# Longer stretches of one kind of matmul in a squared-relu FFN behind a dynamic convolution, and two relus of eight on VectorE

## The chip, the cores and the metric

The kernel runs on one core of one Trainium2 chip. The metric is the device time of one execution in microseconds (us). All times below are medians of several executions; the profiles are of one execution each, and their span (first to last instruction) lies about 2 us below the time of the same execution. The granted clock of a profile is the share of its full clock that TensorE was given; 1 is all of it.

The profile shows five engines of the core, working side by side (in the kernel before TensorE is busy for 98% of the span, ScalarE for 77% and VectorE for 74%): TensorE (PE in the profile; PEld is its loading of weights), VectorE (DVE), ScalarE (ACT), GpSimd (POOL) and SyncE (SP), which here only issues DMA transfers. Where an engine waits, the profile names what ended the wait. VectorE's order, which this case turns on, is that of the program. PSUM is the memory that the matmuls of this program write to and that ScalarE and VectorE read the results from.

## The reference

A softmax over 7 taps per token and head weights a causal convolution of `x`; its result goes through a feed-forward network with a squared relu. Cut to what matters:

```python
batch, seq, d_model = (8, 4096, 192);  n_heads, kernel_size = 8, 7;  d_ff = 2048
w   = softmax(weight_gen, axis=-1)                 # (8, 4096, 8, 7)
out = np.einsum('bshk,bskhg->bshg', w, x_unf)      # x_unf: the last 7 rows of x
x   = out.reshape(B * S, D)                        # (32768, 192)
h   = np.maximum(x @ w_in, 0.0)
return (h * h @ w_out).astype(np.float32)
```

## The kernel before

The 32768 tokens are worked in 64 blocks of 512. For each block TensorE does the convolution (conv) as a product of `x` with a banded matrix, then x @ w_in (MM1), then h*h @ w_out (MM2). MM1 of a block comes as eight pairs of 128-column chunks; each pair fills one PSUM tile of 128x1024 fp32 elements, and there are three such tiles (`ps_h`, bufs=3), shared with the conv. ScalarE takes the relu of a pair out of PSUM, VectorE squares it:

```python
def st_relu(j, fp):
    t1 = p_t1.tile([P, 2, 2, TH], f16, name="t1")
    nc.scalar.activation(out=t1, in_=h_t[(j, fp)], func=ActF.Relu)

def st_sq(j, fp):
    g = p_g.tile([P, 2, 2, TH], f16, name="g")
    nc.vector.tensor_tensor(out=g, in0=t1, in1=t1, op=AluOp.mult)
```

The banded matrices `bd` are made by VectorE: rows of softmax weights (`wr`), read back from device memory (`vd`), times a mask. `wr_load` is that read, issued by SyncE; `o_store`, the write of the finished output, is issued by SyncE too. This is the loop (`j` is the block, `fp` the pair; cut: some cases of the first blocks and the softmax; `#` comments added):

```python
for j in range(NBLK):
    ...
    st_conv(j + 1); st_y_evac(j + 1)
    st_bands(j + 2, 0)              # VectorE: bands for the conv after the next
    for fp in G0:                   # pairs 0..3
        st_mm1(j, fp); st_relu(j, fp); st_sq(j, fp)
    for half in (0, 1):
        st_mm2(j - 1, G1, (half,))  # second half of the block BEFORE
        o_copy(j - 1, half, nc.scalar.copy)
    o_store(j - 1, (0, 1), nc.sync) # in the middle of the block
    st_bands(j + 2, 1)
    ...                             # a part of a later softmax
    for fp in G1:                   # pairs 4..7
        st_mm1(j, fp); st_relu(j, fp); st_sq(j, fp)
    st_mm2(j, G0)
    if j + 3 < NBLK:
        wr_load(j + 3)              # last in the block
```

The softmax here doesn't subtract the row's maximum and nothing guards it: scores larger than these inputs give would overflow.

Of the kernel before, what the change touches and what calls it, by code (L numbers as in the profile page):

```python
# [9 lines left out]
def kernel(  # L10
# [20 lines left out]
    nc = tc.nc  # L31
# [41 lines left out]
    p_wr = ctx.enter_context(tc.tile_pool(name="p_wr", bufs=4))  # L73
    p_bd = ctx.enter_context(tc.tile_pool(name="p_bd", bufs=3))
    p_y = ctx.enter_context(tc.tile_pool(name="p_y", bufs=2))
    p_t1 = ctx.enter_context(tc.tile_pool(name="p_t1", bufs=5))
    p_g = ctx.enter_context(tc.tile_pool(name="p_g", bufs=10))
    p_os = ctx.enter_context(tc.tile_pool(name="p_os", bufs=2))
    p_dr = ctx.enter_context(tc.tile_pool(name="p_dr", bufs=3, space=bass.MemoryType.DRAM))
# [14 lines left out]
    def band_mask():  # L94

        nc.gpsimd.memset(mask, 1.0)
        for sign, base in ((1, 0), (-1, KK - 1)):
            nc.gpsimd.affine_select(
                out=mask, in_=mask, pattern=[[sign, P], [0, 2]], compare_op=AluOp.is_ge,
                fill=0.0, base=base, channel_multiplier=-sign,  # L100
            )
# [2 lines left out]


    WQ = 2
    w_sa, w_sb, wo_st, x_st = {}, {}, {}, {}

    def load_w_in(q):
        n = Dff // WQ  # L110
        c = slice(q * n, (q + 1) * n)
        w_sa[q] = p_st.tile([P, n], f32, name="w_sa")
        w_sb[q] = p_st.tile([P, n], f32, name="w_sb")
        nc.sync.dma_start(out=w_sa[q], in_=moe_w_in[0:P, c])
        for r0 in (0, RT):
            nc.sync.dma_start(out=w_sb[q][r0 : r0 + RT], in_=moe_w_in[P:D, c])

    def cast_w_in(q, straight, crossed):
        n = Dff // WQ
        c = slice(q * n, (q + 1) * n)  # L120
        straight(out=w_i[:, 0, c], in_=w_sa[q])
        crossed(out=w_i[RT:P, 1, c], in_=w_sa[q][0:RT])
        crossed(out=w_i[0:RT, 1, c], in_=w_sa[q][RT:P])
        straight(out=w_i[:, 2, c], in_=w_sb[q])

    def load_w_out(q):
        n = NF // WQ
        wo_st[q] = p_st.tile([P, n, Dm], f32, name="wo_st")
        nc.sync.dma_start(
            out=wo_st[q],  # L130
            in_=moe_w_out[q * n * P : (q + 1) * n * P].rearrange("(c p) m -> p c m", p=P),
        )

    def cast_w_out(q, copy):
        n = NF // WQ
        copy(out=w_o[:, q * n : (q + 1) * n], in_=wo_st[q])  # L136


    class Softmax:
# [113 lines left out]
    def x_load(j):  # L253
        x_t[j] = p_x.tile([P, NT, D], f16, name="xt")
        block_load(j, x_t[j], x[j // NBB], D, nc.gpsimd)

    def x_load_f32(j):
        x_st[j] = p_st.tile([P, NT, D], f32, name="x_st")
        block_load(j, x_st[j], x[j // NBB], D, nc.sync)

    def x_cast(j, copy):
        x_t[j] = p_x.tile([P, NT, D], f16, name="xt")
        copy(out=x_t[j], in_=x_st[j])

    def wr_load(j):
        wr_t[j] = p_wr.tile([P, NT, HP, SL * 2], f16, name="wr")
        wr = wr_t[j].rearrange("p t g c -> p t (g c)")
        block_load(j, wr, vd_t[j // NBB], H * SL, nc.sync)

    def wr_load_sbuf(s, order, engines):  # L270

        wr_t[0] = p_wr.tile([P, NT, HP, SL * 2], f16, name="wr")
        for n, i in enumerate(order):
            t0 = max(starts[i], 0)
            engines[n % len(engines)].dma_start(
                out=wr_t[0][:, i].rearrange("p g c -> p (g c)"),
                in_=s.v[t0 // s.r : (t0 + P) // s.r, HALO : HALO + s.r].rearrange(
                    "p r g c e -> p r (g c e)"
                ),
            )  # L280
# [91 lines left out]

    def st_mm2(j, fps, halves=(0, 1)):

        if fps[0] == 0:
            o_t[j] = [ps_o.tile([P, TB], f32, name=f"o{half}") for half in range(2)]
        o = o_t[j]
        for fp in fps:
            for jj in range(2):
                fc = 2 * fp + jj  # L380
                for half in halves:
                    for cc in range(2):
                        nc.tensor.matmul(  # L383
                            out=o[half][:, cc * Dm : (cc + 1) * Dm],
                            lhsT=g_t[(j, fp)][:, half, jj, cc * P : (cc + 1) * P],
                            rhs=w_o[:, fc, :],
                            start=(fc == 0 and cc == 0), stop=(fc == NF - 1),
                            skip_group_check=True,
                        )

    def st_relu(j, fp):
        t1 = p_t1.tile([P, 2, 2, TH], f16, name="t1")
        t1_t[(j, fp)] = t1
        nc.scalar.activation(out=t1, in_=h_t[(j, fp)], func=ActF.Relu)  # L394

    def st_sq(j, fp):
        g = p_g.tile([P, 2, 2, TH], f16, name="g")
        g_t[(j, fp)] = g
        t1 = t1_t[(j, fp)]
        nc.vector.tensor_tensor(out=g, in0=t1, in1=t1, op=AluOp.mult)  # L400

    def o_copy(j, half, copy):
        if half == 0:
# [17 lines left out]
            for tiles in (groups, ((NT - 1,),))[part]:  # L421
                st_band(j, tiles)

    G0, G1 = (0, 1, 2, 3), (4, 5, 6, 7)
    UNIT = 4

    with nc.allow_low_precision("fp16 matmul pipeline"), tc.manual_schedule():
# [12 lines left out]
        def spin(n):  # L440
            for i in range(n):
                nc.tensor.matmul(  # L442
                    out=wp[:, 0:TB], lhsT=warm[:, 0:P], rhs=warm, start=True, stop=True
                )

        spin(38)
        band_mask()
        nc.gpsimd.memset(v_first[2], 0.0)
        nc.gpsimd.memset(v_big, 0.0)
        vec, act, pool = nc.vector.tensor_copy, nc.scalar.copy, nc.gpsimd.tensor_copy  # L450

        def softmax(s, lo, hi):
            s.exp(lo, hi)
            s.recip(lo, hi)
            s.scale(lo, hi, nc.vector)

        s0, s1, s2 = parts
        s0.load(nc.sync)
        s1.load(nc.sync)
        x_load_f32(0)  # L460
        load_w_in(0)
        load_w_in(1)
        s0.exp(0, s0.rh)
        s1.exp(0, s1.rh)
        x_cast(0, act)
        s0.recip(0, s0.rh)
        s0.scale(0, s0.rh, nc.vector)
        s1.recip(0, s1.rh)
        wr_load_sbuf(s0, (0, 2, 1, 3, 4), (nc.scalar, nc.gpsimd))
        s0.store(nc.scalar)  # L470
        cast_w_in(0, act, pool)
        wr_load(1)
        x_load_f32(1)
        load_w_out(0)
        for i in (0, 2, 1, 3, 4):
            st_band(0, (i,))
        st_conv_alloc(0)
        st_conv(0)
        spin(4)
        st_y_evac(0)  # L480
        s1.scale(0, s1.rh, nc.vector)
        s1.store(nc.sync)
        cast_w_in(1, pool, pool)
        x_cast(1, pool)
        wr_load(2)
        x_load(2)
        load_w_out(1)
        for q in range(WQ):
            cast_w_out(q, pool)
        s2.load(nc.sync)  # L490
        st_bands(1, 0)
        st_bands(1, 1)


        plan = {}
# [16 lines left out]
        for j in range(NBLK):  # L512
            nb, lo, hi = plan.get(j, (None, 0, 0))
            after = plan.get(j + 1)
            if after and after[1] == 0:
                s = Softmax(after[0], 0, R, v_big, new_vd(after[0]))
                s.load(nc.sync)
                rows_of[after[0]] = s
            if j + 3 < NBLK:
                x_load(j + 3)  # L520

            late = j == 2
            if j:
                if j + 1 < NBLK:
                    st_conv_alloc(j + 1)
                    st_conv(j + 1)
                    st_y_evac(j + 1)
                if not late:
                    st_bands(j + 2, 0)
            for fp in G0:  # L530
                st_mm1(j, fp)
                st_relu(j, fp)
                st_sq(j, fp)
            if j:
                for half in (0, 1):
                    st_mm2(j - 1, G1, (half,))
                    o_copy(j - 1, half, nc.scalar.copy)
                o_store(j - 1, (0, 1), nc.sync)
            elif NBLK > 1:
                st_conv_alloc(1)  # L540
                st_conv(1)
                st_y_evac(1)
                st_bands(2, 0)
            if not late:
                st_bands(j + 2, 1)
            if hi and j:
                s = rows_of[nb]
                softmax(s, lo, hi)
                if hi == s.rh:
                    s.store(nc.sync)  # L550
            for fp in G1:
                st_mm1(j, fp)
                st_relu(j, fp)
                st_sq(j, fp)
            st_mm2(j, G0)
            if hi and not j:
                softmax(rows_of[nb], lo, hi)
            if late:
                st_bands(j + 2, 0)
                st_bands(j + 2, 1)  # L560
            if j + 3 < NBLK:
                wr_load(j + 3)
        st_mm2(NBLK - 1, G1, (0,))
        o_copy(NBLK - 1, 0, nc.scalar.copy)
        st_mm2(NBLK - 1, G1, (1,))
        o_store(NBLK - 1, (0,), nc.sync)
        o_copy(NBLK - 1, 1, nc.vector.tensor_copy)
        o_store(NBLK - 1, (1,), nc.scalar)
# [30 lines left out]
```

## Time and profile before

| | before |
|---|---|
| time, median of 3 (range) | 794.05 us (792.2 to 794.29) |
| span of the profile, granted TensorE clock | 791.0 us, 0.993 |
| TensorE busy | 773.3 us, 98% |
| ScalarE, VectorE busy | 77%, 74% |
| one block, conv to conv | 11.78 us, or 11.89 where ScalarE does a long exp for a later softmax |

TensorE is busy 98% of the time, at a clock of 0.993, so the span is its stream of instructions. The prediction below shows the lines.

### The profile page before, as it was taken

To read this page: it belongs to the slowest core of one execution; us is meant where nothing else is said; L and a number is where in the kernel's file an instruction comes from. 1 tells how busy PE (TensorE), PEld (TensorE's weight loads), DVE (VectorE), ACT (ScalarE), POOL (GpSimd) and SP (SyncE) were. 2 spreads that over 40 slices of the span, in tenths; PEclk is the share of its full clock that TensorE was granted. 3 is DMA by queue.
4 is the path that set the end of the run, shared out by engine and by line. 5 is a ranking of instruction groups with operands and counts; after the bars stand their busy time and mean duration, and the time that the engine had idled before them with its cause. 6 is when DMAs were issued, how large, how long until landed. Compare 5 with 4: busy or idle time off the path is not lost.

```text
span 791.0 us, 32666 instructions
## 1 busy us (share of the span) xinstructions
PE 773.3 (98%) x14890; PEld 679.7 (86%) x14890; DVE 586.7 (74%) x1040; ACT 605.4 (77%) x756; POOL 81.8 (10%) x98
## 2 busy tenths in 40 slices
PE   5998999999999999999999999999999999999998
PEld 2787888888888888888988888888888888888887
DVE  5888777777877768777778777877778777666653
ACT  3676877877877877877877877887787787787785
POOL 7501000010001000010001000011000010000000
PEclk9999999999999999999999999999999999999999
DMA  7862633435433543435433353333533334342111
GB/s 197 227 111 38 157 52 64 75 53 145 75 52 65 102 104 65 74 52 148 73 51 67 72 135 67 70 55 68 150 60 65 65 64 89 65 69 46 50 42 41
DMA packets 124009, 65.64 MB, mean 83 GB/s; under 512 B 84545, under 2 KB 121056, under 8 KB 123104
## 3 DMA queue, kind: packets, MB, share of 16 engines
q1 hardware_dynamic: 82032, 47.92, 21.6%
q0 software_dynamic: 40992, 15.28, 18.5%
q8 instruction: 116, 1.90, 1.1%
q10 hardware_dynamic: 848, 0.38, 0.2%
q14 instruction: 21, 0.17, 0.1%
HBM read 49.35 MB, written 29.36 MB: 100 GB/s over the span
## 4 chain that ended last, share of the span: by engine, by line
PE 93%; DMA 3%; DVE 2%; ACT 1%; issue 0%; SPq 0%; ACTq 0%; DVEq 0%
PE o L383 44%; PE h L364 43%; PE yp L339 6%; DMA wg<-in_weight_gen_dram 1%; DVE bd L290 1%; DMA wr<-v_first 1%; DMA x_st<-in_x_dram 1%; DMA vd<-v_first 0%; DVE g L400 0%; ACT t L394 0%; DVE v_big L194 0%; ACT ex L173 0%; DVE v_first L194 0%; DVE ssum L181 0%; DVE rcp L186 0%
## 5 line engine op out<-in xcount | busy, mean ns | idle before, releaser
L394 ACT ACTIVATE t<-h 128x1024 f16<-128x1024 f32 x512 | 482.8, 1031 | 9.4 <-PE h L364 8.8
L400 DVE TENSOR_TENSOR g<-t 128x1024 f16<-128x1024 f16 x512 | 346.9, 692 | 147.1 <-ACT t L394 146.9
L364 PE MATMUL h<-y,w_i 64*128 64x256 f16 x6144 | 362.5, 270 | 2.0 <-ACT y L352 1.2
L383 PE MATMUL o<-w_o,g 128*128 128x192 f16 x4096 | 360.0, 246 | 0.0
L383 PEld LDWEIGHTS <-g 128*128 128x128 f16 x4096 | 331.5, 98 | 26.8 <-DVE g L400 17.1
L364 PEld LDWEIGHTS <-w_i 64*128 64x128 f16 x6144 | 292.4, 94 | 51.0 <-issue 14.2
L290 DVE TENSOR_TENSOR bd<-wr,mask 128x1664 f16<-128x1664 f16 (+2 forms) x201 | 163.4, 844 | 11.2 <-DMA wr<-vd 6.2
L352 ACT CAST y<-yp 128x768 f16<-128x768 f32 x64 | 51.1, 798 | 122.8 <-PE yp L339 122.8
L251 POOL DMA_DIRECT2D xt<-in_x_dram x62 | 51.2, 826 | 460.4 <-PE yp L339 437.0
L405 ACT COPY o_sb<-o 128x384 f32<-128x384 f32 x127 | 62.9, 495 | 38.3 <-PE o L383 38.3
L339 PE MATMUL yp<-bd,xt 128*32 128x104 f16 (+13 forms) x4608 | 59.9, 203 | 10.6 <-DVE bd L290 10.5
L339 PEld LDWEIGHTS <-xt 128*32 128x32 f16 (+3 forms) x4608 | 51.2, 91 | 21.6 <-issue 21.5
L181 DVE TENSOR_REDUCE ssum<-ex 128x64 f32<-128x448 f32 (+6 forms) x49 | 25.9, 529 | 35.4 <-ACT ex L173 35.4
L194 DVE TENSOR_TENSOR v_big<-ex,rcp 128x112 f16<-128x112 f32 (+3 forms) x192 | 32.7, 234 | 1.6
L173 ACT ACTIVATE ex<-wg 128x448 f32<-128x448 f32 (+6 forms) x49 | 26.5, 541 | 5.0 <-DMA wg<-in_weight_gen_dram 4.9
L186 DVE RECIPROCAL rcp<-ssum 128x64 f32<-128x64 f32 (+6 forms) x49 | 23.3, 475 | 1.7
L245 POOL DMA_DIRECT2D xt<-in_x_dram x9 | 5.0, 552 | 85.2 <-PE yp L339 85.2
L442 PE MATMUL wp<-warm 128*128 128x512 f16 x42 | 12.4, 463 | 1.3 <-DVE warm L434 1.3
L241 POOL DMA_DIRECT2D xt<-in_x_dram x7 | 3.8, 541 | 77.5 <-PE yp L339 77.5
L442 PEld LDWEIGHTS <-warm 128*128 128x128 f16 x42 | 4.6, 114 | 7.9 <-issue 3.7
L194 DVE TENSOR_TENSOR v_first<-ex,rcp 128x112 f16<-128x112 f32 (+2 forms) x32 | 5.5, 242 | 0.2
L136 POOL CAST w_o<-wo_st 128x1536 f16<-128x1536 f32 x2 | 3.7, 1826 | 5.7 <-DMA wo_st<-in_moe_w_out_dram 5.7
(22 smaller groups left out, 25.5 us busy)
## 6 DMA issues: line engine op xcount, KB each, us to landing
out_dram<-o_sb SPq DMA_DIRECT2D x63, 384.0 KB, 2.8
xt<-in_x_dram POOLq DMA_DIRECT2D x46, 240.0 KB, 4.4
wg<-in_weight_gen_dram SPq DMA_DIRECT2D x6, 1064.0 KB, 6.0
wr<-vd SPq DMA_DIRECT2D x46, 80.0 KB, 3.0
vd<-v_big SPq DMA_DIRECT2D x7, 512.0 KB, 2.9
xt<-in_x_dram POOLq DMA_DIRECT2D x16, 192.0 KB, 3.9
wo_st<-in_moe_w_out_dram SPq DMA_DIRECT2D x2, 768.0 KB, 7.5
wr<-vd SPq DMA_DIRECT2D x17, 64.0 KB, 2.9
```

The source lines that it names most:

```text
L173: nc.scalar.activation(out=self.ex[:, lo:hi].rearrange("p r g k e -> p (r g) k e"), in_=self.wg[:, lo:hi].rearrange("p r (g e) k -> p (r g ...
L181: nc.vector.tensor_reduce(out=ssum.rearrange("p r g e -> p (r g) e"), in_=self.ex[:, lo:hi].rearrange("p r g k e -> p (r g) e k"), axis=Ax ...
L194: eng.tensor_tensor(out=bass.AP(tensor=v.tensor, offset=v.offset + lo * H * SL + lo % SL * 2 + g * SL * 2, ap=[list(v.ap[0]), [H * SL + 2, ...
L251: eng.dma_start(out=dst[:, first:last], in_=ap)
L290: nc.vector.tensor_tensor(out=bd_t[j][:, H * lo : H * hi].rearrange("p (g m c) -> p g m c", g=shape[1], c=2 * SL), in0=wr_t[j][:, i : tile ...
L339: nc.tensor.matmul(out=yp_t[j][p0 : p0 + m, col + a : col + b], lhsT=x_t[j][:, i, 32 * q : 32 * q + m], rhs=bd[:, h // 2, h % 2, a - lo : ...
L352: nc.scalar.copy(out=y, in_=yp_t[j][:, 0 : NK * TH].rearrange("p (k c) -> p k c", k=NK))
L364: nc.tensor.matmul(out=h[:, half, jj, :], lhsT=w_i[r0 : r0 + RT, slot, fc * P : (fc + 1) * P], rhs=y_t[j][r0 : r0 + RT, k, :], start=(jj = ...
L383: nc.tensor.matmul(out=o[half][:, cc * Dm : (cc + 1) * Dm], lhsT=g_t[(j, fp)][:, half, jj, cc * P : (cc + 1) * P], rhs=w_o[:, fc, :], star ...
L394: nc.scalar.activation(out=t1, in_=h_t[(j, fp)], func=ActF.Relu)
L400: nc.vector.tensor_tensor(out=g, in0=t1, in1=t1, op=AluOp.mult)
L405: copy(out=o_sb_t[j][:, half], in_=o_t[j][half][:, 0 : 2 * Dm])
```

## The change

Its intent is to lose less between kinds of matmul. Before, a block's stream is conv, MM1 (4 pairs), MM2 of the block before, MM1 (4 pairs), MM2: five changes of kind. After, it is conv, MM1 (8 pairs), MM2 (8 pairs): three. Since eight relus in a row would press ScalarE (there they follow at 0.915 us, the pairs of MM1 at 0.655, as the prediction reads from the trace before), VectorE takes the relus of pairs 1 and 4, and ScalarE squares those two. The first loads and casts are reordered as well. The core of the diff (the start, some 100 lines, is cut; so are the buffer counts):

```diff
     def st_relu(j, fp):
-        nc.scalar.activation(out=t1, in_=h_t[(j, fp)], func=ActF.Relu)
+        if swapped:
+            nc.vector.tensor_scalar_max(out=t1, in0=h_t[(j, fp)], scalar1=0.0)
+        else:
+            nc.scalar.activation(out=t1, in_=h_t[(j, fp)], func=ActF.Relu)
...
+    SWAPPED = (1, 4)
+    MM2 = (0, 2, 3, 5, 6, 7, 1, 4)
...
                 if not late:
                     st_bands(j + 2, 0)
-            for fp in G0:
+            for fp in range(NFP):
                 st_mm1(j, fp)
                 st_relu(j, fp)
-                st_sq(j, fp)
-            if j:
-                for half in (0, 1):
-                    st_mm2(j - 1, G1, (half,))
-                    o_copy(j - 1, half, nc.scalar.copy)
-                o_store(j - 1, (0, 1), nc.sync)
...
-            for fp in G1:
-                st_mm1(j, fp)
-                st_relu(j, fp)
+            for fp in SWAPPED:
                 st_sq(j, fp)
-            st_mm2(j, G0)
...
-            if j + 3 < NBLK:
-                wr_load(j + 3)
+            st_mm2(j, MM2[:4])
+            for half in (0, 1):
+                st_mm2(j, MM2[4:], (half,))
+                if more or half == 0:
+                    o_copy(j, half, nc.scalar.copy)
+            if more:
+                o_store(j, (0, 1), nc.sync)
+                if j + 3 < NBLK:
+                    wr_load(j + 3)
```

More of the change, by code (lines that the diff above doesn't have):

```diff
@@ L75 @@
     p_y = ctx.enter_context(tc.tile_pool(name="p_y", bufs=2))
-    p_t1 = ctx.enter_context(tc.tile_pool(name="p_t1", bufs=5))
+    p_t1 = ctx.enter_context(tc.tile_pool(name="p_t1", bufs=6))
+    p_t1s = ctx.enter_context(tc.tile_pool(name="p_t1s", bufs=2))
     p_g = ctx.enter_context(tc.tile_pool(name="p_g", bufs=10))
@@ L106, with cast_w_in, load_w_out @@
     WQ = 2
-    w_sa, w_sb, wo_st, x_st = {}, {}, {}, {}
+    NQ = Dff // WQ
+    w_sa, w_sb, x_st = {}, {}, {}
     def load_w_in(q):
-        n = Dff // WQ
-        c = slice(q * n, (q + 1) * n)
-        w_sa[q] = p_st.tile([P, n], f32, name="w_sa")
-        w_sb[q] = p_st.tile([P, n], f32, name="w_sb")
+        c = slice(q * NQ, (q + 1) * NQ)
+        w_sa[q] = p_st.tile([P, NQ], f32, name="w_sa")
+        w_sb[q] = p_st.tile([RT, NQ], f32, name="w_sb")
         nc.sync.dma_start(out=w_sa[q], in_=moe_w_in[0:P, c])
-        for r0 in (0, RT):
-            nc.sync.dma_start(out=w_sb[q][r0 : r0 + RT], in_=moe_w_in[P:D, c])
-    def cast_w_in(q, straight, crossed):
-        n = Dff // WQ
-        c = slice(q * n, (q + 1) * n)
-        straight(out=w_i[:, 0, c], in_=w_sa[q])
-        crossed(out=w_i[RT:P, 1, c], in_=w_sa[q][0:RT])
-        crossed(out=w_i[0:RT, 1, c], in_=w_sa[q][RT:P])
-        straight(out=w_i[:, 2, c], in_=w_sb[q])
-    def load_w_out(q):
-        n = NF // WQ
-        wo_st[q] = p_st.tile([P, n, Dm], f32, name="wo_st")
-        nc.sync.dma_start(
-            out=wo_st[q],
-            in_=moe_w_out[q * n * P : (q + 1) * n * P].rearrange("(c p) m -> p c m", p=P),
-        )
-    def cast_w_out(q, copy):
-        n = NF // WQ
-        copy(out=w_o[:, q * n : (q + 1) * n], in_=wo_st[q])
+        nc.sync.dma_start(out=w_sb[q], in_=moe_w_in[P:D, c])
+    def cast_w_in(q, op, copy):
+        c = slice(q * NQ, (q + 1) * NQ)
+        lower, upper = slice(0, RT), slice(RT, P)
+        out_p, slot, src = {
+            "straight": (slice(0, P), 0, w_sa[q]),
+            "up": (upper, 1, w_sa[q][lower]),
+            "down": (lower, 1, w_sa[q][upper]),
+            "last": (lower, 2, w_sb[q]),
+            "last up": (upper, 2, w_sb[q]),
+        }[op]
+        copy(out=w_i[out_p, slot, c], in_=src)
+    def load_w_out(q, n):
+        nc.gpsimd.dma_start(
+            out=w_o[:, q * NF // n : (q + 1) * NF // n],
+            in_=moe_w_out[q * Dff // n : (q + 1) * Dff // n].rearrange(
+                "(c p) m -> p c m", p=P
+            ),
+        )
     class Softmax:
@@ L268, in wr_load, with wr_load_sbuf @@
         block_load(j, wr, vd_t[j // NBB], H * SL, nc.sync)
-    def wr_load_sbuf(s, order, engines):
-        wr_t[0] = p_wr.tile([P, NT, HP, SL * 2], f16, name="wr")
+    def wr_load_sbuf(j, s, order, engines):
+        wr_t[j] = p_wr.tile([P, NT, HP, SL * 2], f16, name="wr")
         for n, i in enumerate(order):
-            t0 = max(starts[i], 0)
+            t0 = max(j * TB + tile_start(j, i), 0)
             engines[n % len(engines)].dma_start(
-                out=wr_t[0][:, i].rearrange("p g c -> p (g c)"),
+                out=wr_t[j][:, i].rearrange("p g c -> p (g c)"),
                 in_=s.v[t0 // s.r : (t0 + P) // s.r, HALO : HALO + s.r].rearrange(
@@ L373, in st_mm2 @@
     def st_mm2(j, fps, halves=(0, 1)):
-        if fps[0] == 0:
+        if fps[0] == MM2[0]:
             o_t[j] = [ps_o.tile([P, TB], f32, name=f"o{half}") for half in range(2)]
@@ L386, in st_mm2 @@
                             rhs=w_o[:, fc, :],
-                            start=(fc == 0 and cc == 0), stop=(fc == NF - 1),
+                            start=(fp == MM2[0] and jj == 0 and cc == 0),
+                            stop=(fp == MM2[-1] and jj == 1),
                             skip_group_check=True,
@@ L391, in st_relu @@
     def st_relu(j, fp):
-        t1 = p_t1.tile([P, 2, 2, TH], f16, name="t1")
+        swapped = fp in SWAPPED
+        t1 = (p_t1s if swapped else p_t1).tile([P, 2, 2, TH], f16, name="t1")
         t1_t[(j, fp)] = t1
-        nc.scalar.activation(out=t1, in_=h_t[(j, fp)], func=ActF.Relu)
+        if swapped:
+            nc.vector.tensor_scalar_max(out=t1, in0=h_t[(j, fp)], scalar1=0.0)
+        else:
+            nc.scalar.activation(out=t1, in_=h_t[(j, fp)], func=ActF.Relu)
     def st_sq(j, fp):
@@ L399, in st_sq @@
         t1 = t1_t[(j, fp)]
-        nc.vector.tensor_tensor(out=g, in0=t1, in1=t1, op=AluOp.mult)
+        if fp in SWAPPED:
+            nc.scalar.activation(out=g, in_=t1, func=ActF.Square)
+        else:
+            nc.vector.tensor_tensor(out=g, in0=t1, in1=t1, op=AluOp.mult)
     def o_copy(j, half, copy):
@@ L422, in st_bands @@
                 st_band(j, tiles)
-    G0, G1 = (0, 1, 2, 3), (4, 5, 6, 7)
+    SWAPPED = (1, 4)
+    MM2 = (0, 2, 3, 5, 6, 7, 1, 4)
     UNIT = 4
@@ L444, in spin @@
                 )
-        spin(38)
-        band_mask()
-        nc.gpsimd.memset(v_first[2], 0.0)
-        nc.gpsimd.memset(v_big, 0.0)
-        vec, act, pool = nc.vector.tensor_copy, nc.scalar.copy, nc.gpsimd.tensor_copy
         def softmax(s, lo, hi):
@@ L455, in softmax @@
             s.scale(lo, hi, nc.vector)
+        vec, act, pool = nc.vector.tensor_copy, nc.scalar.copy, nc.gpsimd.tensor_copy
         s0, s1, s2 = parts
+        spin(36)
+        band_mask()
         s0.load(nc.sync)
-        s1.load(nc.sync)
-        x_load_f32(0)
         load_w_in(0)
         load_w_in(1)
+        x_load_f32(0)
         s0.exp(0, s0.rh)
-        s1.exp(0, s1.rh)
-        x_cast(0, act)
         s0.recip(0, s0.rh)
         s0.scale(0, s0.rh, nc.vector)
-        s1.recip(0, s1.rh)
-        wr_load_sbuf(s0, (0, 2, 1, 3, 4), (nc.scalar, nc.gpsimd))
-        s0.store(nc.scalar)
-        cast_w_in(0, act, pool)
-        wr_load(1)
-        x_load_f32(1)
-        load_w_out(0)
+        cast_w_in(0, "straight", act)
+        cast_w_in(0, "up", act)
+        cast_w_in(0, "down", pool)
+        cast_w_in(0, "last", act)
+        cast_w_in(0, "last up", act)
+        wr_load_sbuf(0, s0, (0, 1, 2, 4, 3), (nc.sync, nc.gpsimd))
+        cast_w_in(1, "up", vec)
+        cast_w_in(1, "down", vec)
+        x_load(1)
+        s1.load(nc.sync)
+        for q in range(4):
+            load_w_out(q, 4)
+        nc.gpsimd.memset(v_first[2], 0.0)
+        x_cast(0, act)
+        wr_load_sbuf(1, s0, range(NT), (nc.sync,))
+        s0.store(nc.sync)
+        s2.load(nc.sync)
+        cast_w_in(1, "straight", act)
+        cast_w_in(1, "last", act)
         for i in (0, 2, 1, 3, 4):
@@ L479 @@
         spin(4)
+        s1.exp(0, s1.rh)
         st_y_evac(0)
+        cast_w_in(1, "last up", act)
+        x_load(2)
+        nc.gpsimd.memset(v_big, 0.0)
+        st_bands(1, 0)
+        st_bands(1, 1)
+        s1.recip(0, s1.rh)
         s1.scale(0, s1.rh, nc.vector)
         s1.store(nc.sync)
-        cast_w_in(1, pool, pool)
-        x_cast(1, pool)
         wr_load(2)
-        x_load(2)
-        load_w_out(1)
-        for q in range(WQ):
-            cast_w_out(q, pool)
-        s2.load(nc.sync)
-        st_bands(1, 0)
-        st_bands(1, 1)
         plan = {}
@@ L522 @@
             late = j == 2
+            more = j + 1 < NBLK
             if j:
-                if j + 1 < NBLK:
+                if more:
                     st_conv_alloc(j + 1)
@@ L529 @@
                     st_bands(j + 2, 0)
-            for fp in G0:
+            for fp in range(NFP):
                 st_mm1(j, fp)
                 st_relu(j, fp)
-                st_sq(j, fp)
-            if j:
-                for half in (0, 1):
-                    st_mm2(j - 1, G1, (half,))
-                    o_copy(j - 1, half, nc.scalar.copy)
-                o_store(j - 1, (0, 1), nc.sync)
-            elif NBLK > 1:
+                for sq in {3: (0,), 7: (2, 3, 5, 6, 7)}.get(fp, ()):
+                    st_sq(j, sq)
+            if not j and more:
                 st_conv_alloc(1)
@@ L543 @@
                 st_bands(2, 0)
-            if not late:
-                st_bands(j + 2, 1)
-            if hi and j:
+            if late:
+                st_bands(j + 2, 0)
+            st_bands(j + 2, 1)
+            if hi:
                 s = rows_of[nb]
@@ L550 @@
                     s.store(nc.sync)
-            for fp in G1:
-                st_mm1(j, fp)
-                st_relu(j, fp)
+            for fp in SWAPPED:
                 st_sq(j, fp)
-            st_mm2(j, G0)
-            if hi and not j:
-                softmax(rows_of[nb], lo, hi)
-            if late:
-                st_bands(j + 2, 0)
-                st_bands(j + 2, 1)
-            if j + 3 < NBLK:
-                wr_load(j + 3)
-        st_mm2(NBLK - 1, G1, (0,))
-        o_copy(NBLK - 1, 0, nc.scalar.copy)
-        st_mm2(NBLK - 1, G1, (1,))
+            st_mm2(j, MM2[:4])
[3 more added lines that the diff above has]
+                    o_copy(j, half, nc.scalar.copy)
+            if more:
+                o_store(j, (0, 1), nc.sync)
+                if j + 3 < NBLK:
+                    wr_load(j + 3)
         o_store(NBLK - 1, (0,), nc.sync)
```

## The prediction

> **What bounds the kernel now.** I read the page first: busy shares, then the chain that ended last.
>
> ```profile
> PE 773.3 (98%) x14890; PEld 679.7 (86%) x14890; DVE 586.7 (74%) x1040; ACT 605.4 (77%) x756; POOL 81.8 (10%) x98
> PE 93%; DMA 3%; DVE 2%; ACT 1%; issue 0%; SPq 0%; ACTq 0%; DVEq 0%
> ```
>
> TensorE carries 93% of the chain: a gain must make its stream shorter. VectorE and ScalarE are below 80%, so off the path on average. Then the timeline of one steady block (columns: start us, us, engine, line, operation, count):
>
> ```profile
> 401.99 2.90 PE L364 MATMUL h<-y,w_i 64*128 64x256 f16 x48
> 402.47 0.63 ACT L173 ACTIVATE ex<-wg 128x448 f32<-128x448 f32 x1
> 402.99 3.76 ACT L394 ACTIVATE t<-h 128x1024 f16<-128x1024 f32 x4
> 404.83 2.81 PE L383 MATMUL o<-w_o,g 128*128 128x192 f16 x32
> 407.57 0.91 PE L339 MATMUL yp<-bd,xt 128*32 128x104 f16 x72
> 408.41 2.79 PE L364 MATMUL h<-y,w_i 64*128 64x256 f16 x48
> 408.57 0.80 ACT L352 CAST y<-yp 128x768 f16<-128x768 f32 x1 [1.82 <-PE yp L339]
> 409.28 3.77 ACT L394 ACTIVATE t<-h 128x1024 f16<-128x1024 f32 x4
> 411.13 2.81 PE L383 MATMUL o<-w_o,g 128*128 128x192 f16 x32
> ```
>
> By differences of starts, a block is conv 0.84, MM1 2.72, MM2 2.75, MM1 2.72 (2.84 here, where a softmax exp precedes the relus), MM2 2.74: 11.78, or 11.89 with such an exp. There is no idle time inside, but a little is lost where one kind follows another. The end of the kernel shows how much:
>
> ```profile
> 776.28 2.81 PE L383 MATMUL o<-w_o,g 128*128 128x192 f16 x32
> 781.75 5.45 PE L383 MATMUL o<-w_o,g 128*128 128x192 f16 x64
> ```
>
> 32 more MM2 matmuls in the same stretch cost 5.45 - 2.81 = 2.64 us, yet a stretch of 32 takes 2.74 to 2.75 from its start to the next stretch: 0.10 is the switch. For MM1: 2.79 less the last matmul's mean 0.27 leaves 2.52 for 23 steps of a row-tile pair, 0.1095 each; 24 steps are 2.63, and the stretch takes 2.72: switch 0.09. A chunk pair of MM1 (6 such steps) is 0.655.
>
> The groups by shape give the unit costs that I use (the two numbers after the bar are busy us and mean ns):
>
> ```profile
> L394 ACT ACTIVATE t<-h 128x1024 f16<-128x1024 f32 x512 | 482.8, 1031 | 9.4 <-PE h L364 8.8
> L400 DVE TENSOR_TENSOR g<-t 128x1024 f16<-128x1024 f16 x512 | 346.9, 692 | 147.1 <-ACT t L394 146.9
> L405 DVE COPY o_sb<-o 128x384 f32<-128x384 f32 x1 | 0.6, 557 | 2.9 <-PE o L383 2.9
> ```
>
> Four relus take 3.77, so they follow at (3.77 - 1.03)/3 = 0.915.
>
> [...] MM1 is 64x128, MM2 128x128, conv 128x32; [...] I estimate 1.22 us for the new VectorE relu, against ScalarE's 1.03. [...] The trace has one table load (1.28 us), and the built changed program still has one, so Square costs none. Its duration I estimate as that of the ScalarE cast of 1024 elements from SBUF in the trace, 1.045, following at about 0.93.
>
> **The change, part by part.**
>
> *Fewer switches.* Per block five changes of kind become three: -0.19 us, x 64 = -12. Ideal block: MM1 16 x 3 x 0.1095 + 0.1 = 5.36, MM2 64 x 0.0825 + 0.1 = 5.39, conv 0.84: 11.59.
>
> *PSUM slots.* MM1 results have three slots, shared with conv. Two groups of four pairs, with MM2 between, let them drain; eight pairs in a row reuse them at once. A slot is refilled every third pair, 3 x 0.655 = 1.96. Its round is: pair 0.655, until the relu starts 0.215 (a relu with nothing ahead of it starts 0.87 after its pair: MM1 at 779.02, relu at 779.89), relu, and about 0.04 to the next matmul. With ScalarE: 1.94, just fits, which is why MM1 shows no stall now. With VectorE: 2.13. Pairs 1 and 4 are VectorE's, and in the built program's PSUM addresses, in 53 of 63 blocks with a conv, pairs 1, 4, 7 share a slot: two waits of 0.17. By hand from MM1's start: relu 1 from 1.52 to 2.75; pair 4 at 2.79 (not 2.62); relu 2 at 2.18; relu 3 at 3.09, so pair 6 at 4.16; relu 4 from 3.65 to 4.88; pair 7 at 4.91 (not 4.58). Stall 0.336, x 64 = +21.5. In 9 blocks the addresses differ: pair 4 takes pair 2's slot, freed at 3.21, and pair 7 pair 4's; the same working gives 0.80, so +0.46 x 9 = +4.
>
> *ScalarE's tail.* Relu 7 starts at 6.14; the squares of pairs 1 and 4 come after it and after any exp. MM2 starts at 5.69 and wants square 4 at 5.69 + 4 x 0.66 + 3 x 0.33 = 9.32. Without exp it is ready at 6.14 + 0.915 + 0.93 + 1.045 = 9.03. An 8-row exp (0.62, delays by 0.52) makes it 9.55: with about 0.1 to load the weights, a stall of about 0.32; a 4-row exp (0.41) 0.1. With 18 of each (groups by shape): +8. Before, such exps cost 18 x 0.11 = 2.
>
> *VectorE's load.* Per block it trades two squares (0.60 spacing) for two relus: about +1.2, near 10.5 of 11.9 in a block with softmax. From the durations it finishes the next conv's bands 1.4 us before relu 1 needs it: off the path when steady.
>
> *Start.* Now the first MM1 begins at 23.0, because the stationary bands wait for 15.1 (small loads behind 3.4 MB) and take 5.5 where GpSimd casts run beside them. Afterwards some 2.5 MB precede those loads at the 227 GB/s that the page shows, so bands at about 13.3, for about 4 us: first MM1 about 19 (-4). Of stalls around 36, 43, 58 to 61, 63 to 72 us in the present start (9 us, with a half-clock stretch from 63.8 to 67.2), the load-to-store trip of the softmax rows is better hidden. But VectorE does the second softmax part before relu 1 of block 0 (I estimate +2.2), and collides in blocks 1 and 3 (+1 and +2); the longer exps of the first blocks add 2 to 2.5[...]: about 9 again.
>
> *Sum.* First MM1 19, 64 x 10.75 + 63 x 0.84 = 741, tail after the last matmul 3.8 as now, slots 25.5, exps 8, start 9: 806. The same sum for before gives 23 + 753 + 3.8 + 2 + 9 = 791, its span, so the bookkeeping closes. Measured times lie 2 to 3 above the span. That would be 808; because each stall is an upper estimate (a stall taken by one wait partly hides the next), I say 804.
>
> **The rivals.** (1) TensorE's stream wins: the slot waits are hidden[...]. Then about -12 from switches and -4 from the start: 778 to 786. For it: VectorE is 74% busy, the stall per relu is only 0.17. Against: 1.94 against 1.96 leaves ScalarE no slack to give back[...]. (2) VectorE becomes the bound in softmax blocks: at 10.5 of 11.9, a band late by 1.5 us would hold relu 1, thus PSUM, thus TensorE; 0.5 us in half the blocks makes 820. Against: 1.4 us of slack by hand. (3) Only the start matters (-4 to -10) and steady blocks cancel: about 788.
>
> **Range and chances.** Main uncertainties: relu duration (30 ns is 2 x 30 x 64 = 4 us), the exps (4), the start (5). I take 804 with 789 to 814. Faster by 2% is below 778.2: every stall would have to vanish, 5%. Slower by 2% is above 809.9: 22%. Within: 73%.
>
> **What would show it.** VectorE relu near 1.22 us; MM1 stretch of 96 at 5.6 to 5.7 rather than 5.36, with TensorE waits named VectorE's relu at pairs 4 and 7; MM2 stretch of 64 at 5.39 without exp and near 5.7 with; period about 11.93 without exp (now 11.78), 12.2 with 8-row exps; first MM1 near 19. The prediction is wrong if the MM1 stretch is near 5.36 (slots not binding), if relu 1 starts late because VectorE is still on bands, or if the start gains over 8 us.

## The result and the profile after

| | before | after |
|---|---|---|
| time, median of 4 (range) | 794.17 us (792.2 to 795.34) | 1184.1 us (1181.56 to 1188.44) |
| span, granted clock | 791.0 us, 0.993 | 1179.6 us, 0.874 |
| TensorE busy | 773.3 us | 885.6 us |
| TensorE idle (span less busy) | 17.7 us | 294.0 us |

The changed kernel takes 1.492 times as long (95% interval 1.487 to 1.497). A ratio here is the mean time of one kernel's fast runs over that of the other's of the same rounds, so not quite the ratio of the medians.

Of the 388.6 us that the span grew, 276.3 are idle time of TensorE and 112.3 are time in which it is busy for longer. This is the page of the kernel after: busy time of each engine, granted TensorE clock in 40 slices (tenths), shares by engine of the chain that ended last (followed back from the last instruction, at each step to what released it), and groups of instructions (after the bar: busy us, mean ns; then the idle us just before them and what ended most of it).

```profile
PE 885.6 (75%) x14888; PEld 772.9 (66%) x14888; DVE 636.1 (54%) x1042; ACT 640.7 (54%) x761; POOL 74.1 (6%) x96
...
PEclk9888888888888888988889888888988988888889
...
PE 52%; DMA 22%; DVE 12%; issue 6%; ACT 5%; SPq 3%; DVEq 0%; ACTq 0%
...
L364 PE MATMUL h<-y,w_i 64*128 64x256 f16 x6144 | 471.4, 319 | 284.2 <-DVE t L397 279.9
...
L290 DVE TENSOR_TENSOR bd<-wr,mask 128x1664 f16<-128x1664 f16 (+2 forms) x201 | 161.8, 834 | 424.9 <-DMA wr<-vd 421.2
...
L397 DVE TENSOR_SCALAR t<-h 128x1024 f16<-128x1024 f32 x128 | 156.3, 1221 | 57.2 <-PE h L364 57.2
```

And two of the same groups in the page of the kernel before:

```profile
L364 PE MATMUL h<-y,w_i 64*128 64x256 f16 x6144 | 362.5, 270 | 2.0 <-ACT y L352 1.2
...
L290 DVE TENSOR_TENSOR bd<-wr,mask 128x1664 f16<-128x1664 f16 (+2 forms) x201 | 163.4, 844 | 11.2 <-DMA wr<-vd 6.2
```

No engine is busy for more than 75%, yet the span is half as long again: most of this is waiting, not work. Two new waits stand out. TensorE waits 279.9 us in MM1 for VectorE's relu (L397), and VectorE waits 421.2 us for the `wr` rows before it can make bands (L290), against 6.2 before. Transfers, which had 3% of the chain before, have 22%. The relu itself is innocent of size: 1221 ns, as estimated. MM1's 6144 matmuls, the same ones, are busy for 471.4 us in place of 362.5, which is 109 of the 112 us of longer busy time.

How the two waits hang together shows in the chain of one block of the kernel after (columns: start us, us, what):

```profile
606.34 0.49 ACT o_sb L413
...
606.85 0.38 SPq L418
...
607.27 3.20 DMA wr<-vd
...
611.43 1.02 DVE bd L290
612.45 1.15 DVE t L397
...
613.64 4.46 PE h L364 x48
618.10 5.45 PE o L383 x64
...
623.57 0.49 ACT o_sb L413
```

This is a closed loop. The copy of the finished output at the end of a block (606.34) lets SyncE issue the output store (L418). Only behind it does SyncE issue the load of `wr`, which lands 3.20 us later. VectorE then makes two bands (from 610.49), then relu 1 (L397). That relu frees the PSUM tile for the second half of MM1, then comes MM2, and then the next copy of an output, 17.23 us after the first. The pieces shown sum to 16.15; the first band, which the chain counts as issue time, and small gaps are the rest. So the loop is the whole period. TensorE's own 11.6 us no longer set it.

The timeline of the same block shows what TensorE does meanwhile (in brackets: idle time of the engine just before, and who ended it):

```profile
607.08 2.84 PE L364 MATMUL h<-y,w_i 64*128 64x256 f16 x48
...
607.27 0.51 SPq L251 DMA_DIRECT2D wr<-vd  x1
...
610.49 1.96 DVE L290 TENSOR_TENSOR bd<-wr,mask 128x1664 f16<-128x1664 f16 x2 [5.33 <-DMA wr<-vd]
612.37 1.22 DVE L397 TENSOR_SCALAR t<-h 128x1024 f16<-128x1024 f32 x1
...
613.64 4.46 PE L364 MATMUL h<-y,w_i 64*128 64x256 f16 x48 [3.72 <-DVE t L397]
```

TensorE does four pairs (48 matmuls, 2.84 us) and stops, since pair 4 needs the tile of pair 1. The relu of pair 1 could start 1.6 us after MM1 (as it does in the second experiment), at about 608.7, but begins at 612.37. It stands behind the bands in VectorE's order, and did not pass them: VectorE is idle for 5.33 us up to 610.49, although for the last 1.8 of them this relu was at hand.

After 3.72 us of idling the next 48 matmuls take 4.46 us in place of 2.84. The view by windows gives the granted clock there (columns: window, us, busy us of PE, PEld, DVE, ACT, POOL with counts, PEclk, DMA share, GB/s):

```profile
613.64:616.80 3.16, 3.16 (x34) 2.80 (x35) 2.59 (x4) 0.76 (x1) 0.00 (x0) 0.57 0.00 0
```

The clock was 0.57 there, and 0.50 in the part from 614.60 to 617.00, after a wait of 3.72 us. Over the whole trace, the 60 stretches of MM1 that follow a wait of over 3 us have a mean clock of 0.59 and run at 92 ns per matmul on average; all other stretches of MM1 have 0.997, and the first stretches of the blocks mostly run at 55 ns. So the wait is paid twice: 279.9 us of waiting, then 109 us of MM1 at a lower clock.

Now the kernel before, same view, one block:

```profile
402.60 0.38 SPq L410 DMA_DIRECT2D out_dram<-o_sb  x1
...
403.03 0.50 SPq L251 DMA_DIRECT2D wr<-vd  x1
...
407.53 1.95 DVE L290 TENSOR_TENSOR bd<-wr,mask 128x1664 f16<-128x1664 f16 x2
```

SyncE does the same there: store, then load 0.43 us behind it. But that store is the one of block j-1, which is finished in the middle of the block, so the load is issued 4.5 us ahead of the bands and costs nothing. Merging the two stretches of MM2 moved the end of each block's output, hence the store, hence the load, from the middle to the end of the block. The line `wr_load(j + 3)` stands last in the loop in both kernels, and in both SyncE issues one store and then one load per block. But the store ahead of it was that of block j-1 and is now that of block j: the load has slipped behind a store that it used to precede.

### The profile page after: what moved, and what is told of

Same layout as the page of the kernel before. It is cut to its first block, busy times and chain, and to the rows that moved or that the text cites. A ratio compares the mean times of both kernels' runs of the same rounds, so it can differ in the third digit from the quotient of the medians.

```text
span 1179.6 us, 32605 instructions
## 1 busy us (share of the span) xinstructions
PE 885.6 (75%) x14888; PEld 772.9 (66%) x14888; DVE 636.1 (54%) x1042; ACT 640.7 (54%) x761; POOL 74.1 (6%) x96
## 4 chain that ended last, share of the span: by engine, by line
PE 52%; DMA 22%; DVE 12%; issue 6%; ACT 5%; SPq 3%; DVEq 0%; ACTq 0%
PE o L383 28%; PE h L364 24%; DMA wr<-vd 21%; DVE t L397 6%; DVE bd L290 5%; ACT o_sb L413 2%; SPq L418 2%; ACT g L406 1%; ACT t L399 1%; SPq L245 1%; DMA wr<-v_first 0%; ACT ex L173 0%; DVE v_first L194 0%; SPq L275 0%; SPq L241 0%
## 5 line engine op out<-in xcount | busy, mean ns | idle before, releaser
L364 PE MATMUL h<-y,w_i 64*128 64x256 f16 x6144 | 471.4, 319 | 284.2 <-DVE t L397 279.9
L364 PEld LDWEIGHTS <-w_i 64*128 64x128 f16 x6144 | 380.7, 111 | 357.2 <-issue 300.8
L399 ACT ACTIVATE t<-h 128x1024 f16<-128x1024 f32 x384 | 379.7, 1023 | 395.2 <-PE h L364 394.9
L290 DVE TENSOR_TENSOR bd<-wr,mask 128x1664 f16<-128x1664 f16 (+2 forms) x201 | 161.8, 834 | 424.9 <-DMA wr<-vd 421.2
L383 PE MATMUL o<-w_o,g 128*128 128x192 f16 x4096 | 356.0, 248 | 1.6 <-ACT g L406 1.5
L383 PEld LDWEIGHTS <-g 128*128 128x128 f16 x4096 | 337.3, 99 | 23.7 <-issue 17.7
L408 DVE TENSOR_TENSOR g<-t 128x1024 f16<-128x1024 f16 x384 | 251.9, 686 | 46.5 <-ACT t L399 46.4
L397 DVE TENSOR_SCALAR t<-h 128x1024 f16<-128x1024 f32 x128 | 156.3, 1221 | 57.2 <-PE h L364 57.2
L406 ACT ACTIVATE g<-t 128x1024 f16<-128x1024 f16 x128 | 128.1, 1056 | 0.0
L339 PE MATMUL yp<-bd,xt 128*32 128x104 f16 (+12 forms) x4608 | 59.1, 202 | 3.0 <-ACT xt L263 2.6
L245 POOL DMA_DIRECT2D xt<-in_x_dram x10 | 5.8, 583 | 136.3 <-PE yp L339 136.3
L452 PE MATMUL wp<-warm 128*128 128x512 f16 x40 | 12.2, 475 | 1.3 <-DVE warm L444 1.3
```

What stands on the lines that cost most here:

```text
L290: nc.vector.tensor_tensor(out=bd_t[j][:, H * lo : H * hi].rearrange("p (g m c) -> p g m c", g=shape[1], c=2 * SL), in0=wr_t[j][:, i : tile ...
L339: nc.tensor.matmul(out=yp_t[j][p0 : p0 + m, col + a : col + b], lhsT=x_t[j][:, i, 32 * q : 32 * q + m], rhs=bd[:, h // 2, h % 2, a - lo : ...
L364: nc.tensor.matmul(out=h[:, half, jj, :], lhsT=w_i[r0 : r0 + RT, slot, fc * P : (fc + 1) * P], rhs=y_t[j][r0 : r0 + RT, k, :], start=(jj = ...
L383: nc.tensor.matmul(out=o[half][:, cc * Dm : (cc + 1) * Dm], lhsT=g_t[(j, fp)][:, half, jj, cc * P : (cc + 1) * P], rhs=w_o[:, fc, :], star ...
L397: nc.vector.tensor_scalar_max(out=t1, in0=h_t[(j, fp)], scalar1=0.0)
L406: nc.scalar.activation(out=g, in_=t1, func=ActF.Square)
```

## The experiments

My theory after the result: the load stuck behind the output store, with relu 1 behind the bands that wait for it, is the cause. The rivals, with the letters of the expectations: the two VectorE relus among eight pairs in a row cost the time whatever the load does (A); the long stretches lower the clock by themselves (B); the late load does its harm wherever it is waited for (C); VectorE's lateness by itself costs as much, with or without relus on it (D). Further runs measure the small terms of the predicted sum. Every run gave correct results and was timed in three rounds; the kernel before had medians of 793.85 us (first four runs) and 793.69 us (last four) beside them.

### The load ahead of the output store

```diff
+            if j + 3 < NBLK:
+                wr_load(j + 3)
             for fp in SWAPPED:
                 st_sq(j, fp)
             st_mm2(j, MM2[:4])
...
-                if j + 3 < NBLK:
-                    wr_load(j + 3)
```

> The changed kernel with one edit: the load of the stationary rows (wr) for the block after next is issued before the second MM2 stretch, ahead of the store of the block's output, not behind it. My theory (late load: VectorE is in order, its bands wait for the load, relu 1 stands behind the bands, PSUM slots run out, TensorE idles and its clock halves): the bands no longer wait for wr, the clock returns to about 0.99, and the time is what my prediction's other steps give, 795 to 812 us. Rival A (a VectorE relu of 1.22 us on three PSUM slots is itself what stalls TensorE): still over 1000 us. Rival B (the long stretches lower the clock by themselves): the clock stays below 0.9 and the time over 900 us.

Measured: 823.83 us (823.25 to 824.97), 1.038 times the kernel before (1.036 to 1.039), clock 0.994. Moving two lines gives back 360 of the 390 us with the relus where they were, so the late load is needed for the loss; rivals A and B fall. But the run is 12 us above my range. VectorE's waits for `wr` fell from 421.2 us to 32.5 us, in nine waits, about one for each of the eight times that softmax rows are stored:

```profile
187.76 0.33 SPq L208 DMA_DIRECT2D vd<-v_big  x1
188.14 0.43 SPq L245 DMA_DIRECT2D wr<-vd  x1
...
191.65 1.96 DVE L290 TENSOR_TENSOR bd<-wr,mask 128x1664 f16<-128x1664 f16 x2 [3.91 <-DMA wr<-vd]
```

In such a block the load stands behind another store, that of the new softmax rows (L208), which VectorE can only finish late in the block. It is the same queue with another store ahead of it, and but for the first of the eight, which is within one batch, no data ties the two: by the program the rows stored are those of the next batch, while the load (L245 is the issue for a batch's last tile) reads those of the present one. TensorE then stops for 1.65 us within MM1, and the period is 13.1 to 17.3 us in those blocks and 12.0 to 12.3 in most others. From the second block on, the MM1 stretches take 17.4 us more in all than in the next run, which has the same MM2: that is the whole 17.5 us between the two times.

### The load left late, the bands behind the relus

Here the load stays behind the store, and what waits for it is moved instead: the bands come after relus and squares in VectorE's order.

```diff
-                if not late:
-                    st_bands(j + 2, 0)
...
-            if late:
+            if j:
                 st_bands(j + 2, 0)
             st_bands(j + 2, 1)
```

> The changed kernel with the load left late, but the bands that wait for it moved behind the relus and squares in VectorE's order. My theory: the wait for wr is over by then, so 795 to 825 us, and TensorE waits for VectorE's relu by only some 0.3 us per block. Rival A (VectorE's relu itself): over 1000 us. Rival C (the late load is harmful in whatever place it is waited for, by way of the next conv): over 900 us.

Measured: 806.3 us (805.52 to 806.93), ratio 1.0155 (1.014 to 1.017), clock 0.996. One steady block:

```profile
402.16 5.85 PE L364 MATMUL h<-y,w_i 64*128 64x256 f16 x96
...
403.75 1.22 DVE L397 TENSOR_SCALAR t<-h 128x1024 f16<-128x1024 f32 x1 [1.53 <-PE h L364]
...
407.94 5.74 PE L383 MATMUL o<-w_o,g 128*128 128x192 f16 x64
...
410.05 2.42 DVE L290 TENSOR_TENSOR bd<-wr,mask 128x1664 f16<-128x1664 f16 x3
```

Relu 1 starts 1.59 us after MM1, and MM1 of 96 matmuls takes 5.78 us from its start to MM2's. The bands have moved to 410.05 and are done at 412.47, 1.1 us ahead of the conv that starts at 413.61. The period is 12.01 us without an exp, 12.09 with a 4-row one, 12.30 with an 8-row one. The load is as late as in the kernel after, yet 378 of the 390 us are gone: rivals A and C fall. So the late load is dear because of what stands behind its bands in VectorE's order. That is relu 1, but also the squares, which this edit moves out of the way too; the next run takes the relus off VectorE.

### All relus on ScalarE, the load left late

```diff
-    SWAPPED = (1, 4)
-    MM2 = (0, 2, 3, 5, 6, 7, 1, 4)
+    SWAPPED = ()
+    MM2 = (0, 1, 2, 3, 4, 5, 6, 7)
...
-                for sq in {3: (0,), 7: (2, 3, 5, 6, 7)}.get(fp, ()):
+                for sq in {1: (0,), 3: (1, 2), 7: (3, 4, 5, 6, 7)}.get(fp, ()):
```

> The changed kernel with load and bands left as they are, but all eight relus on ScalarE and all eight squares on VectorE, so that VectorE, late as it is, holds no PSUM slot. My theory: MM1 is paced by ScalarE's 0.915 us per pair (about 6.35 us a stretch), MM2 5.4, conv 0.84: 12.6 us a block, 820 to 860 us, clock near 0.99. Rival D (VectorE's lateness costs the same through late squares): over 1000 us.

Measured: 922.48 us (919.3 to 924.75), ratio 1.162 (1.158 to 1.165). I missed by 62 us. The PSUM tiles no longer hang on VectorE, and MM1 takes 6.37 us in the block below, as worked out (404.07 to 410.44). But the squares stand behind the same bands:

```profile
407.61 1.96 DVE L290 TENSOR_TENSOR bd<-wr,mask 128x1664 f16<-128x1664 f16 x2 [4.41 <-DMA wr<-vd]
...
409.49 4.90 DVE L408 TENSOR_TENSOR g<-t 128x1024 f16<-128x1024 f16 x8
```

All eight squares of the block start after 409.49, where MM2 wants the first at 410.44. In this block that is just in time; in others it is not, and MM2 waits 51.9 us in all for a square, and mostly takes 5.97 us in place of 5.38. Of the 129 us lost, MM1's length explains about 51: (6.37 + 5.39 + 0.84 - 11.8) x 64. So rival D holds in part: the late VectorE costs some 78 us, a fifth of the 390, without any relu on it. The run has one more difference: its eight ScalarE relus share six buffers (`p_t1`), and wait 52.0 us for squares to free one. What share of the 78 that makes is not shown.

### The kernel before with its load late

The opposite test: the kernel before, with the load issued right ahead of the bands that need it and behind the output store. The bands move with it, from the head of the block to behind its first four squares in VectorE's order.

```diff
-                if not late:
-                    st_bands(j + 2, 0)
...
                 o_store(j - 1, (0, 1), nc.sync)
+                if j + 2 < NBLK:
+                    wr_load(j + 2)
+                if not late:
+                    st_bands(j + 2, 0)
...
-            if j + 3 < NBLK:
-                wr_load(j + 3)
```

> The kernel before, with the load of wr issued right ahead of the bands that need it, behind the output's store, so that VectorE waits some 3 us per block for it as in the changed kernel. My theory: its relus are all on ScalarE and MM2 runs on squares of the previous half, so the wait is mostly hidden, but VectorE's 8.9 us of work and 3 us of wait come to about the block's 11.8: 794 to 825 us. Rival D: over 1000 us, as in the changed kernel.

Measured: 863.01 us (860.41 to 868.88), ratio 1.086 (1.084 to 1.088); a miss by 38 us. The view of waits (us in total, times, longest):

```profile
DVE bd L290 <- DMA wr<-vd: 256.1, 65, 10.5
...
PE yp L339 <- DVE bd L290: 54.8, 66, 6.3
```

VectorE waits 3.9 us per block (256.1/65). With its 561 us of work that is 817 of the 867 us of this span: with its waits it has become tighter than TensorE (802.5 us busy), and the conv, which needs the bands, waits 54.8 us for it. I had counted the slack of the bands and not that a wait at the head of VectorE's order takes time from all its work, here 3.9 us per block.

Put together, and compared with the kernel before: the late load in the old order costs 69 us (this run), the new order with VectorE relus and an early load costs 30 (first run), and both at once cost 390. The halves make 99 of it; the rest needs the relu behind the late bands, which closes the loop.

### More changes of kind in the kernel before

Two changes of kind are added per block, by splitting MM1's first four pairs into two and two.

```diff
-            for fp in G0:
+            for fp in G0[:2]:
...
-                for half in (0, 1):
-                    st_mm2(j - 1, G1, (half,))
-                    o_copy(j - 1, half, nc.scalar.copy)
+                st_mm2(j - 1, G1, (0,))
+            for fp in G0[2:]:
+                st_mm1(j, fp)
+                st_relu(j, fp)
+                st_sq(j, fp)
...
+                st_mm2(j - 1, G1, (1,))
```

> The kernel before with its first four MM1 pairs cut in two and half of MM2 put between, so that each block but the first has two more changes of kind on TensorE and the same work. If a change of kind costs the 0.09 to 0.10 us that I read from the trace: 63 x 2 x 0.095 = +12 us, about 806 us. Rival ([...] the longer stretch would have brought nothing): 794 us, the same.

Measured: 809.43 us (807.89 to 810.85), ratio 1.0205 (1.018 to 1.023). The period without an exp is 12.00 us in place of 11.78: 0.11 us for each of the two changes, or 14 us in 64 blocks; blocks with a long exp grew by 0.35, and the time by 15.7. So a change of kind costs what the prediction read from the trace. That taking two away gives 12 us back is seen in the last experiment: its block is 11.59 us, 0.19 less.

### The kernel before with the changed start

The edit puts the changed kernel's loads and casts ahead of the loop of the kernel before (all of the cut part of the diff, nothing else).

> The kernel before with the changed kernel's start (loads, casts, first bands) and its own loop. My prediction gave the start about 4 us (first MM1 near 19 instead of 23 us); with the loop's relus on ScalarE the collisions on VectorE matter less: 785 to 791 us, first MM1 at 18 to 20. Rival (the time is set later by the softmax rows' way through memory, so an earlier first MM1 is given back): 793 to 795 us.

Measured: 794.24 us (792.86 to 795.19), ratio 1.001 (0.999 to 1.003): no gain; it missed my range and is inside the rival's. The timeline of TensorE:

```profile
17.94 2.79 PE L363 MATMUL h<-y,w_i 64*128 64x256 f16 x48
...
33.24 0.27 PE L338 MATMUL yp<-bd,xt 128*32 128x104 f16 x2 [4.36 <-DVE bd L289]
```

MM1 begins at 17.94 in place of 23.01, 5 us earlier. Then a conv waits 4.36 us for bands, and by a conv at 75.95 (76.22 before) only 0.3 us are left. So when TensorE first starts is not what bounds the first blocks here. The bands of the 4.36 us wait take the rival's way, by the chain of this trace: new softmax rows are stored from 24.75 (5.09 us), `wr` is loaded from 29.89 (2.15 us), and the bands start at 32.06.

### The squares ahead of the exp

The second experiment's kernel still loses 0.08 to 0.29 us per block where an exp stands ahead of ScalarE's two squares. This run swaps them.

```diff
+            for fp in SWAPPED:
+                st_sq(j, fp)
             if hi:
                 s = rows_of[nb]
                 softmax(s, lo, hi)
...
-            for fp in SWAPPED:
-                st_sq(j, fp)
```

> e2_bands_behind with ScalarE's two squares ahead of the exp in its order. My step 'ScalarE's tail' says that an 8-row exp costs a wait of 0.3 us in MM2 and a 4-row exp 0.1: 18 x 0.3 + 18 x 0.08, and some 2 us for the longer exps of the first blocks: 9 us less than e2, about 797 us; all steady periods near 12.0. Rival (MM2 waits for something else there): 806 us as e2.

Measured: 795.58 us (795.14 to 796.25), ratio 1.003 (1.0014 to 1.0045), 10.7 us less than the second experiment. The period is 11.94 to 12.01 in all kinds of blocks, and MM2 takes 5.38. What is left above the ideal is MM1, 5.71 in place of 5.36.

### Half relus in half tiles

Each PSUM tile is cut into two half tiles, each freed on its own (the expectation calls them one-bank tiles). For pairs 0 to 3 ScalarE takes the relu of the first half and VectorE that of the second at the same time; of pairs 4 to 7 ScalarE takes both halves. Only pair 3 is squared by ScalarE. The order in MM2 follows.

```diff
-        h = ps_h.tile([P, 2, 2, TH], f32, name="h", tag="h")
+        h = [ps_h.tile([P, 2, TH], f32, name=f"h{i}", tag=f"h{i}") for i in range(2)]
...
+        for half, h in enumerate(h_t[(j, fp)]):
+            if half and fp in SPLIT:
+                nc.vector.tensor_scalar_max(out=t1[:, half], in0=h, scalar1=0.0)
+            else:
+                nc.scalar.activation(out=t1[:, half], in_=h, func=ActF.Relu)
...
+    SPLIT = (0, 1, 2, 3)
+    SWAPPED = (3,)
+    MM2 = (0, 1, 2, 4, 5, 6, 7, 3)
```

> e7_squares_first, but with the PSUM tile of a pair as two one-bank tiles: in pairs 0 to 3 ScalarE takes the relu of one bank while VectorE takes that of the other, pairs 4 to 7 are ScalarE's, and ScalarE squares pair 3 alone. A slot is then held about 0.5 us shorter. If the slots cause the 5.785 us of the MM1 stretch (my step 'PSUM slots'): MM1 falls to 5.4 to 5.5, the period to about 11.6, and the time to 768 to 782 us, below both kernels. Rival (something else paces MM1 in long stretches): MM1 stays above 5.65, 790 us or more.

Measured: 774.46 us (774.24 to 774.93), ratio 0.976 (0.975 to 0.978). This version beats both kernels. One steady block:

```profile
399.41 5.43 PE L363 MATMUL h<-y,w_i 64*128 64x256 f16 x96
...
404.77 5.45 PE L382 MATMUL o<-w_o,g 128*128 128x192 f16 x64
...
410.16 0.91 PE L339 MATMUL yp<-bd,xt 128*32 128x104 f16 x72
```

MM1 takes 5.36 us (399.41 to 404.77), MM2 5.39, and the conv, from the one at 398.57, 0.84: the 11.59 us that the prediction called ideal. A half relu takes 691 ns on VectorE and 620 on ScalarE, where a whole one took 1225 and 1025 in the run above, and a half tile is free that much sooner. TensorE is busy 98% of the 772.5 us.

## Why the prediction was wrong

The prediction was 804 us in a range of 789 to 814. The time was 1184.1.

**The step that failed** is in the part on VectorE's load: "From the durations it finishes the next conv's bands 1.4 us before relu 1 needs it: off the path when steady." I summed VectorE's durations and took it that what it reads is there. I had not worked out when `wr` lands in the new order, though the profile before had what it takes for an estimate: an output copy takes 0.5 us and the conv 0.84, so store and load go out about when MM1 starts; a `wr` load lands 3.0 us after its issue, and two bands take 1.95. That puts relu 1 some 5 us after MM1's start. In the kernel after it is issued 0.42 us behind a store that waits for the block's last copy, and the bands start at 610.49 where MM1 started at 607.08. Relu 1, for which I had "from 1.52", came at 5.29 us after MM1's start. The second experiment, which only moves those bands behind the relus and squares, brings it to 1.59 and the time to 806.3. One of my signs of being wrong had named just this: "if relu 1 starts late because VectorE is still on bands". Rival (2) named this chain (a band late holds relu 1, PSUM, TensorE) but saw a cause in VectorE's amount of work, and gave 0.5 us in half of the blocks. Measured, it was 279.9 us over 62 waits, 4.5 each, in nearly all blocks. I also had no term for the clock: after waits as long as these MM1 ran at a mean clock of 0.59, which cost 109 us more.

**Fewer switches** (-12): right in kind and size; two added changes cost 15.7 us, at 0.11 us each where no exp interferes, and the last experiment's block is the 11.59 us called ideal.

**PSUM slots** (+25.5): right, seen once the bands were out of the way. MM1 took 5.78 and 5.71 for a predicted 5.69, VectorE's relu 1221 to 1225 ns for 1.22 us, which was my estimate: the trace before has no relu on VectorE. Half tiles, which take the waits away, give 21.1 us between the last two experiments (their split of pairs also moves one square to VectorE). The 0.46 us more in 9 blocks with another order of PSUM addresses did not show: in the second experiment MM1 takes 5.78 to 5.79 us in all blocks but the first and one of 6.14. Whether that build has the other order at all is not on record.

**ScalarE's tail** (+8): right; over 5.38 per block, MM2 takes 8.9 us more in all in the second experiment and 0.3 after the swap of squares and exp, which gives 10.7 us in all. The periods of the second experiment, 12.01, 12.09 and 12.30, answer to 11.93 worked out for no exp and 12.2 for an 8-row one.

**Start** (first MM1 4 us earlier, stalls of 9 us as before, so 4 us net in the sum): the first MM1 came at 18.06 us in the kernel after, for about 19. But by itself the changed start gains nothing (794.24 us for 793.69): with the old loop the 4 us were given back, which the sum did not have.

**Sum**: 806 of span, given as a time of 804. The second experiment has a span of 804.3 and a time of 806.3. Its trace splits into first MM1 18.5, stream 741, slots 27, exps 9, tail 3.9, which leaves 5 for the stalls of the first blocks, where I had 9: part of the agreement is luck. It is also not quite the kernel that I predicted, since it has another order on VectorE; but it is what the sum describes, a kernel in which bands make nobody wait.

What stays open: a load issued by another engine than the stores, which should take the waits of the first experiment away if the queue alone makes them, and the start of the kernel before ahead of the fastest loop were not run.

## What to carry to other kernels

When a change moves where a block's output is finished, list what stands behind that output's store on the engine that issues it, and ask of each such transfer when it is now issued and who needs it when; that its line still stands in the same place of the loop does not tell, only the wait ahead of it does. An engine with low busy time is not thereby off the critical path: here VectorE, busy for 54% of the span, waited 421.2 us for late operands and made TensorE wait 279.9. One late operand delayed what stood behind it in VectorE's order (relu 1 came 5.29 us after MM1's start behind the bands, and at 1.59 ahead of them), so put what frees PSUM ahead of what waits for memory. When a change leaves every engine idle for a good part of the time, look for a closed loop in the chain: its pieces add up to the period (here the pieces shown are 16.15 of 17.23 us).
